# Loading bands earlier and reordering the blocks of V in a neighbourhood-attention kernel

## The chip, the cores and the metric

The kernel runs on one core of a Trainium2 chip. The metric is device time in microseconds of one execution, as the median of several runs. Five engines run their own instruction streams in program order: TensorE (PE, with its weight loads as PEld), VectorE (DVE), ScalarE (ACT), GpSimd (POOL) and SyncE (SP), which here does nothing but issue DMAs. ACT and POOL issue some DMAs as well.

## The reference

```python
H = W = 224; C = 192; ks, dil = 7, 2
qkv = x @ wqkv                       # x: 224 x 224 x 192, bf16
q, k, v = qkv[..., :C], qkv[..., C:2*C], qkv[..., 2*C:]
r0 = clip(i - 6, 0, H - 1 - 12); c0 = clip(j - 6, 0, W - 1 - 12)
rows, cols = r0 + 2 * arange(7), c0 + 2 * arange(7)
logits = einsum('bnc,bnkc->bnk', q, k[rows, cols]) * C ** -0.5
o = einsum('bnk,bnkc->bnc', softmax(logits), v[rows, cols]) @ wo
```

Each pixel attends to 7 x 7 neighbours at a distance of two rows and two columns. So pixels of one row parity and one column parity form an image of their own, 112 x 112.

## The kernel before

**Steps and pairs.** There are 14 steps `n`, numbered from 0: seven row tiles `ti` of 16 rows by two row classes `rc` (`rc = n % 2`). Each step has 7 pairs `m` of column slots `s = 2m, 2m + 1`, so 98 pairs `k` in all. A pair goes through stages: `stage1` (logits on TensorE, L500; the row maxima on VectorE, L502), `stage1b` (the exponentials on ScalarE, L510), `stage2` (transposes of the probabilities, L529, copied by L530), `stage3` (probabilities times V, L539) and `stage4` (reciprocal L545, scaling L562 into a tile `o_sb`, and the store, L568). In the loop body of pair `k`, `stage3` and `stage4` are those of pair `k - 2`. There are six `o_sb` tiles and each pair writes two.

**Preparation.** While step `n` runs, its pairs also prepare step `n + 1`: the folded queries `G` (`g_items`, L424, evacuated by L334 and on the GpSimd side by L459) and the 14 blocks of V, two a pair (`v_item`, L341 and L344, the cast by `evac`, L334 on ScalarE or L332 on VectorE). A block is 8 columns of a row class.

**VF and VD.** `VF[rc]` holds V of two bands of 8 rows on its lower and upper 64 partitions. `VD[rc]` holds the band before and the lower one. It is filled by DMAs from `VF`: `vd_low` (L355) copies the old upper half of VF to the lower half of VD, and must have read it before new blocks are cast over it; `vd_high` (L358) copies the new lower half of VF to the upper half of VD. `AT` says in which place of the tiles each block lies, so that one DMA can take neighbouring places. Before, blocks 0 to 6 lie at places 0 to 6, block 13 at 7 and blocks 7 to 12 at 8 to 13. In steps 1 to 12 `vd_low` of the other class goes out as seven blocks in pair 1, and `vd_low` of the own class as four and three blocks in pairs 4 and 5. `vd_high` goes out after the eighth block (pair 3) and after the last (pair 6).

**Loads.** `load_items(b)` brings band `b` of x (16 image rows) in three transposing DMAs (L155): two into the rings `XA`, one into `X1`, which has two buffers. Before, in pair 0 of step `n` band `n + 3` is put in `ld`, and each of the pairs 0, 1 and 2 issues one of its three. GpSimd then copies the band into `XB` (`xb_items`) and sorts it into strips `XS` (`sort_items`), from which the blocks of V are made.

**Order.** Everything is emitted by hand in program order and kept so on each engine (`in_order`). SP's queue takes, in a pair, the stores of `stage4`, then `vd_low`, then a load, then `vd_high`. SP issues one DMA after the other; one whose data are not ready holds up those behind it. The DMAs of SP and ACT use eight completion semaphores in turn, so each waits for the DMA eight before it. Step 0 follows a written `PLAN` (V: blocks of its own V, W: blocks of the next step, G and H: queries, R and T: `vd_high`, N: the second `stage4` of a pair, X: `xb_items`). In step 0 the `vd_high` marked `Ta` and the `vd_low` of pairs 4 and 6 are issued by ACT. Step 0 also has transfers of marks in pairs 3 to 6 (`marks_on`, L240).

Of the kernel before, what the change touches and what calls it, by code (L numbers as in the profile page):

```python
# [22 lines left out]
NSTEP = 14  # L23
NBAND = 14
# [3 lines left out]
BND = 16 * S  # L28
C = 192
VP = 2 * C + 2  # L30
AT = (0, 1, 2, 3, 4, 5, 6, 8, 9, 10, 11, 12, 13, 7)
NEG = -1.0e30


# [33 lines left out]
def _win(t, p0, pn, off, dims):  # L68
    a = t[:]
    ps = a.ap[0][0]  # L70
    return bass.AP(a.tensor, a.offset + p0 * ps + off, [[ps, pn]] + [list(d) for d in dims])
# [28 lines left out]
def kernel(  # L100
# [7 lines left out]
    nc = tc.nc  # L108
# [26 lines left out]
    VF = [pers.tile([128, NSLOT, VP], BF, name=f"vf{rc}") for rc in range(2)]  # L135
    VD = [pers.tile([128, NSLOT, VP], BF, name=f"vd{rc}") for rc in range(2)]
# [9 lines left out]
    def load_items(b):  # L146

        src = xp[16 * b:16 * b + 16].rearrange("r j c -> (r j) c")
        at = (16 * b) % (2 * RP) * S

        def one(k):
            if k == 1:
                X1[b] = x1_p.tile([128, BND], BF, name=f"x1_{b}", tag="x1")
            dst = X1[b][:] if k == 1 else XA[k // 2][:, at:at + BND]
            nc.sync.dma_start_transpose(out=dst.unsqueeze(1), in_=src[:, 128 * k:128 * k + 128])  # L155

        return [lambda k=k: one(k) for k in ((0, 2, 1) if b in (0, 2, 3) else (1, 0, 2))]

    def xb_items(b, eng):
        at = (16 * b) % (2 * RP) * S  # L160
# [46 lines left out]
    for cc in range(2):  # L207
        t = pers.tile([128, S], BF, name=f"ch{cc}")
# [121 lines left out]
    def evac(out_, in_, dve):  # L330
        if dve:
            nc.vector.tensor_copy(out=out_, in_=in_)  # L332
        else:
            nc.scalar.copy(out=out_, in_=in_)  # L334
# [11 lines left out]
    def v_item(rc, cb):  # L346
        def emit(dve):
            pv = ps_g.tile([128, 512], F32, name="pv", tag="pg")
            v_mms(pv, lambda k, h: XS[rc][:, k, cb, 64 * h:64 * h + 64])
            evac(_win(VF[rc], 0, 128, AT[cb] * VP, [[193, 2], [1, C]]), pv[:, 0:2 * C].rearrange("p (t c) -> p t c", c=C), dve)  # L350
        return emit

    def vd_low(rc, c0, c1, eng=nc.sync):

        eng.dma_start(out=VD[rc][0:64, c0:c1, 0:VP - 1], in_=VF[rc][64:128, c0:c1, 0:VP - 1])  # L355

    def vd_high(rc, c0, c1, eng=nc.sync):
        eng.dma_start(out=VD[rc][64:128, c0:c1, 0:VP - 1], in_=VF[rc][0:64, c0:c1, 0:VP - 1])  # L358


    def v_first(j):
        def emit(dve):
            pv = ps_g.tile([128, 512], F32, name="pv", tag="pg")
            v_mms(pv, lambda k, h: _win(XS[1], 0, 128, k * NSLOT * 128 + 64 * AT.index(2 * j + h), [[1, 64]]))
            evac(_win(VF[1], 0, 128, (7 + j) * VP, [[193, 2], [1, C]]), pv[:, 0:2 * C].rearrange("p (t c) -> p t c", c=C), dve)
        return emit

    def first_sort(eng):
# [1 line left out]

    def first_vd():
        for u in range(2):
            nc.sync.dma_start(out=_win(VD[1], 0, 64, u * VP, [[2 * VP, 7], [1, VP]]), in_=VF[1][64 * u:64 * u + 64, 7:14, :])


    def row_runs(rc, ti):
# [155 lines left out]
    def stage3(J, ab):  # L532
# [3 lines left out]
        for cc in range(2):  # L536
            for q in range(2):
                for h in range(2):
                    nc.tensor.matmul(o_ps[64 * h:64 * h + 64, cc * 193:cc * 193 + 193], lhsT=J.pt[:, 4 * ab + 2 * cc + q, 64 * h:64 * h + 64],  # L539
                                     rhs=V[h][:, AT[(s - 1 + q) % NSLOT], cc * C:cc * C + 193], start=(q == 0), stop=(q == 1))  # L540
        J.o_ps[ab] = o_ps
# [53 lines left out]
    for n, (ti, rc) in enumerate(steps):  # L595
        for m in range(7):
            J = Pair()
# [4 lines left out]
    def g_all(n):  # L602
# [3 lines left out]

    act, dve, pool = nc.scalar.copy, nc.vector.tensor_copy, nc.gpsimd.tensor_copy
    PLAN = (
        "Va:0 Vd:1 Va:2 Vd:3 Va:4 Vd:5 Va:6 Vd:7 R-:0:8 Va:8 Gd:2 Ga:3 X-",
        "Va:9 Vd:10 X- Va:11 Vd:12 Va:13 R-:8:14 Gd:4 Ga:5",  # L610
        "Gd:6 N- Ga:7 Wa:0 Wd:1 Wa:2",
        "Hd:0 N- Ha:1 Wa:3 Wa:4 Wd:5",
        "Hd:2 N- Ha:3 Wa:6 Wa:7 Ta:0:8 Wd:8",
        "Hd:4 N- Ha:5 Wa:9 Wa:10 Wd:11",
        "Hd:6 N- Ha:7 Wa:12 Wa:13 Ta:8:14",
    )
    pool_q = []
    end_q = []
# [11 lines left out]
    for it in load_items(2):  # L630
        it()
# [11 lines left out]
    t = ps_t.tile([128, 8, 128], BF, name="pt_ps", tag="pt")  # L643
# [13 lines left out]
    ld = []  # L657

    for k in range(NP + 2):
        J = pairs[k] if k < NP else None  # L660
        n = J.n if J else NSTEP
        w64, w128 = [], []
        if J:
            m = J.m
            if m == 0 and n + 1 < NSTEP:
                rc1 = steps[n + 1][1]
                gw, gh = g_all(n + 1)
                vs = [v_item(rc1, cb) for cb in (0, 1, 2, 3, 4, 5, 6, 13, 7, 8, 9, 10, 11, 12)]
            if n == 0:
                w64 = (gh0 + gh)[m + 1:m + 2]  # L670
            elif n + 1 < NSTEP:
                w128 = gw[m + (m > 1):m + 1 + (m > 0)] + vs[2 * m:2 * m + 2]
                w64 = gh[m // 2:m // 2 + 1] if m % 2 == 0 else []
            stage1(J, 0)
            stage1(J, 1)
            stage1b(J, 0)
            if m == 0 and n + 3 < NBAND:
                ld = load_items(n + 3)
        if k == NP:
            stage2(pairs[k - 1])  # L680
        if k >= 2:
            stage3(pairs[k - 2], 0)
            stage3(pairs[k - 2], 1)
            if k >= NP:
                stage4a(pairs[k - 2], 0)
                stage4a(pairs[k - 2], 1)
            stage4(pairs[k - 2], 0)
            if k == NP - 1:
                stage4a(pairs[k - 2], 1)
        for it in w64:  # L690
            it(False)
        if J:
            stage1b(J, 1)
        if 1 <= k < NP:
            stage2(pairs[k - 1])

        if k >= 2 and n > 0:
            stage4(pairs[k - 2], 1)
        if not J:
            continue  # L700

        if m == 1 and 0 < n and n + 1 < NSTEP:
            vd_low(rc1, 7, 14)
        if n == 0 and m in (4, 6):
            vd_low(0, *((0, 4) if m == 4 else (4, 7)), nc.scalar)
        if 0 < n and m in (4, 5) and n + 2 < NSTEP:
            vd_low(J.rc, *((0, 4) if m == 4 else (4, 7)))
        if ld:
            ld.pop(0)()
        for w in PLAN[m].split() if n == 0 else ():  # L710
            (kind, by), at = w.split(":")[0], [int(c) for c in w.split(":")[1:]]
            if kind in "VWGH":
                {"V": v0, "W": vs, "G": gw0, "H": gw}[kind][at[0]](by == "d")
            elif kind == "N" and k >= 2:
                stage4(pairs[k - 2], 1)
            elif kind == "X":
                xb2.pop(0)()
            elif kind == "R":
                vd_high(0, at[0], at[1], nc.scalar if by == "a" else nc.sync)
            elif kind == "T":  # L720
                vd_high(rc1, at[0], at[1], nc.scalar if by == "a" else nc.sync)
        for it in w128:
            it(False)
            if it is vs[7]:
                vd_high(rc1, 0, 8)
            if it is vs[13]:
                vd_high(rc1, 8, 14)
        if n == 0 and m == 0:
            for q in range(2):
                marks(q, 2 * MM, 2 * MM + 3, pool)  # L730
        if n == 0 and m == 1:
            first_vd()
            g_row_on(1, 2, 12)
            g_col_on()
        if n == 0 and m >= 3:
            marks_on(m % 2, 2 * MM + 3 + (m - 3) // 2)
        add = []
        if n == 0:
            add = {0: sort_items(1, 1, pool), 1: sort_items(2, 1, pool), 3: sort_items(2, 0, pool), 4: xb_items(3, pool) + sort_items(3, 0, pool)}.get(m, [])
        else:  # L740
            if m == 0 and n + 2 < NBAND:
                add = sort_items(n + 2, J.rc, pool)

            if m in ((2, 4) if n > 1 else (3,)) and n + 3 < NBAND:
                srt = sort_items(n + 3, J.rc, pool)
                one, two = xb_items(n + 3, pool) + srt[2:], srt[:2]
                add = (two if m == 4 else one) if n > 1 else one + two
        pool_q[:0] = add
        if n == 1 and m == 1:
            g_col(0, 1, 0, 1, pool)  # L750
            g_row(0, 1, 0, 1, pool, ((0, 16, MM - 6, 1),))
            g_row(0, 1, 1, 13, pool, ((0, 6, MM - 6, 1),))
        if n == 12 and m == 1:
            last = ((0, 9, 0, 1), (9, 7, 9, 0))
            g_col(1, 6, 0, 1, pool)
            g_row(1, 6, 0, 1, pool, last)
            g_row(1, 6, 1, 13, pool, last[1:])
        pool_do(5 if n == 1 and m == 3 else 4)
# [34 lines left out]
```

## Time and profile before

| | us |
|---|---|
| median of 3 runs | 360.83 |
| the runs | 360.83, 363.97, 360.31 |
| the profiled execution | 362.43 |
| its span | 360.7 |
| PE, PEld busy | 332.8, 302.4 |
| DVE, ACT, POOL busy | 314.0, 312.3, 281.0 |
| DMA moved | 60.05 MB, mean 167 GB/s |

The span runs from the first to the last instruction; the profiled execution's own time is 1.7 us more. Busy time is that of an engine's own work, and matmuls are pipelined, so that TensorE's busy time isn't TensorE at its peak. A group of instructions carries the line of kernel.py that issued it; `evac` and the stages are helpers, so one line stands for many places in the loop. SPq is SP's queue of DMA issues.

### The profile page before, as it was taken

The page shows a single profiled execution, that of the slowest core. Times are in us where ns is not written, and L with a number is a line of the kernel's source. Part 1 is how long each engine was busy: PE and PEld are TensorE (multiplying, and loading weights), DVE is VectorE, ACT ScalarE, POOL GpSimd, SP SyncE. Part 2 cuts the span into 40 slices and gives each one's busy share as a digit, 9 for nine tenths or more (in the row PEclk, how much of TensorE's full clock was granted, in tenths as well). Part 3 has the DMA queues.
Part 4 walks back from the last instruction along what each step waited for, and adds up shares of the span by engine and source line. Part 5 has one row for each costly group of instructions (what it writes and reads, how often), then busy time and mean ns, then how long its engine had stood idle before and what let it go on. Part 6 is the DMA issues. An engine that isn't in the chain of part 4 may idle for free.

```text
span 360.7 us, 18676 instructions
## 1 busy us (share of the span) xinstructions
PE 332.8 (92%) x7714; PEld 302.4 (84%) x7714; DVE 314.0 (87%) x743; ACT 312.3 (87%) x825; POOL 281.0 (78%) x446
## 2 busy tenths in 40 slices
PE   4686999989999998999999999999999999999872
PEld 2575878879998897899987999889999999999762
DVE  8977999878998888789987899898998989989893
ACT  7854779799999896999989999999999989999893
POOL 8595799999996977959959699696996878274182
PEclk9998999999999999999999999999999999999999
DMA  8997776899978969889699897998979955645423
GB/s 192 210 175 110 172 169 162 142 209 191 182 160 183 195 153 179 204 165 192 154 175 207 170 208 177 205 188 200 202 171 199 176 136 118 151 97 121 101 66 91
DMA packets 136768, 60.05 MB, mean 167 GB/s; under 512 B 88706, under 2 KB 136159, under 8 KB 136684
## 3 DMA queue, kind: packets, MB, share of 16 engines
q1 hardware_dynamic: 129412, 55.73, 76.1%
q0 software_dynamic: 5280, 1.71, 2.7%
q10 hardware_dynamic: 1992, 1.44, 2.0%
q8 instruction: 60, 0.98, 1.2%
q14 instruction: 24, 0.20, 0.1%
HBM read 0.29 MB, written 19.27 MB: 54 GB/s over the span
## 4 chain that ended last, share of the span: by engine, by line
PE 69%; DVE 11%; ACT 10%; DMA 4%; issue 4%; DVEq 0%; ACTq 0%
PE s L500 16%; PE o_ps L539 13%; PE pg L424 9%; PE pv L341 9%; PE pt_ps L529 8%; PE pv L344 7%; ACT p L510 7%; PE pgh L424 5%; DMA vd<-vf 4%; DVE nmx L502 3%; DVE o_sb L562 2%; ACT gx L334 1%; ACT g L334 1%; DVE g L332 1%; DVE pt_sb L530 1%
## 5 line engine op out<-in xcount | busy, mean ns | idle before, releaser
L510 ACT ACTIVATE p<-s,nmx 128x224 bf16<-128x224 f32 x392 | 150.9, 455 | 22.3 <-DVE nmx L502 20.3
L502 DVE TENSOR_REDUCE nmx<-s 128x2 f32<-128x392 f32 (+1 forms) x196 | 102.6, 565 | 21.0 <-PE s L500 19.5
L459 POOL COPY g<-gx 64x512 bf16<-64x512 bf16 (+1 forms) x110 | 62.3, 566 | 48.1 <-ACT gx L334 44.2
L334 ACT CAST vf<-pv 128x384 bf16<-128x384 f32 x193 | 88.6, 528 | 12.5 <-DMA vd<-vf 8.1
L562 DVE TENSOR_TENSOR o_sb<-o_ps,rs 128x384 bf16<-128x384 f32 x169 | 94.2, 558 | 5.9
L591 POOL DMA_DIRECT2D out_dram<-o_s x150 | 84.6, 571 | 9.4 <-DVE rs L545 7.8
L341 PE MATMUL pv<-wb,xs 128*64 128x384 bf16 x406 | 72.7, 333 | 14.0 <-ACT gx L334 5.5
L539 PE MATMUL o_ps<-vd,pt_sb 128*64 128x193 bf16 x784 | 81.6, 246 | 2.3 <-ACT pt_sb L530 2.1
L500 PE MATMUL s<-xa,g 128*64 128x196 bf16 (+7 forms) x990 | 82.6, 233 | 1.2 <-ACT p L510 0.7
L500 PE MATMUL s<-xb,g 128*64 128x196 bf16 (+7 forms) x990 | 82.3, 233 | 0.3 <-ACT g L334 0.3
L539 PE MATMUL o_ps<-vf,pt_sb 128*64 128x193 bf16 x784 | 81.7, 246 | 0.0
L500 PEld LDWEIGHTS <-g 128*64 128x64 bf16 x1980 | 78.1, 111 | 3.2 <-issue 1.6
L539 PEld LDWEIGHTS <-pt_sb 128*64 128x64 bf16 x1568 | 71.3, 109 | 3.8 <-ACT pt_sb L530 3.1
L344 PE MATMUL pv<-wp,xs 128*64 128x192 bf16 x812 | 73.0, 249 | 0.0
L530 DVE COPY pt_sb<-pt_ps 128x1024 bf16<-128x1024 bf16 x92 | 63.2, 687 | 5.7 <-PE pt_ps L529 0.6
L344 PEld LDWEIGHTS <-xs 128*64 128x64 bf16 x812 | 60.1, 111 | 8.2
L529 PE MATMUL pt_ps<-ident,p 128*64 128x128 bf16 x1552 | 63.8, 219 | 0.0
L529 PEld LDWEIGHTS <-p 128*64 128x64 bf16 x1552 | 57.1, 110 | 4.9
L334 ACT CAST g<-pg 128x512 bf16<-128x512 f32 (+4 forms) x136 | 58.0, 474 | 2.5 <-PE pg L424 2.3
L424 PEld LDWEIGHTS <-aw 128*64 128x64 bf16 x1320 | 55.2, 111 | 3.3
L424 PE MATMUL pg<-xb,aw 128*64 128x512 bf16 (+9 forms) x440 | 54.9, 271 | 0.0
L341 PEld LDWEIGHTS <-xs 128*64 128x64 bf16 x406 | 33.7, 111 | 23.3 <-issue 14.4
(77 smaller groups left out, 383.8 us busy)
## 6 DMA issues: line engine op xcount, KB each, us to landing
out_dram<-o_sb SPq DMA_DIRECT2D x156, 96.0 KB
vd<-vf SPq DMA_DIRECT2D x13, 385.0 KB
vd<-vf SPq DMA_DIRECT2D x12, 336.9 KB
vd<-vf SPq DMA_DIRECT2D x13, 288.8 KB
vd<-vf SPq DMA_DIRECT2D x11, 192.5 KB
vd<-vf SPq DMA_DIRECT2D x11, 144.4 KB
out_dram<-o_s POOLq DMA_DIRECT2D x78, 9.0 KB, 3.1
out_dram<-o_sb SPq DMA_DIRECT2D x13, 78.0 KB
```

Of the source, the lines that this page charges most:

```text
L334: nc.scalar.copy(out=out_, in_=in_)
L341: nc.tensor.matmul(pv[64 * h:64 * h + 64, 0:2 * C], lhsT=at(1, h), rhs=WB[:].rearrange("p t c -> p (t c)"), start=True, stop=False, skip_g ...
L344: nc.tensor.matmul(pv[64 * h:64 * h + 64, cc * C:(cc + 1) * C], lhsT=at(2 * cc, h), rhs=WP[(cc, 0)], start=False, stop=True, skip_group_ch ...
L424: nc.tensor.matmul(o, lhsT=l, rhs=r, start=(pas == 0), stop=(pas == 1))
L500: nc.tensor.matmul(o, lhsT=w, rhs=r, start=(pas == 0), stop=(pas == 1))
L502: nc.vector.tensor_reduce(out=nmx[:], in_=_win(s_ps, 0, 128, lo, [[256, 2], [16, 14], [1, 16 - lo]]), axis=AX.XY, op=ALU.max, negate=True)
L510: nc.scalar.activation(out=J.p[:, ab, cc, :, z:z + 112].rearrange("p q (r k) -> p q r k", k=8), in_=_win(s_ps, 0, 128, cc * 256, [[8, 2], ...
L529: nc.tensor.transpose(pt_ps[64 * h:64 * h + 64, 4 * ab + 2 * cc + q, :], J.p[:, ab, cc, q, 64 * h:64 * h + 64], ident[:])
L530: (nc.scalar.copy if J.n == NSTEP - 1 and J.m < 5 else nc.vector.tensor_copy)(out=J.pt[:], in_=pt_ps[:])
L539: nc.tensor.matmul(o_ps[64 * h:64 * h + 64, cc * 193:cc * 193 + 193], lhsT=J.pt[:, 4 * ab + 2 * cc + q, 64 * h:64 * h + 64], rhs=V[h][:, A ...
L562: nc.vector.tensor_tensor(out=o_sb[:], in0=_win(o_ps, 0, 128, 0, [[194, 2], [1, C]]), in1=rs[:].unsqueeze(2).to_broadcast([128, 2, C]), op ...
L591: pool_q.append(lambda dst=dst, p=p, m=n * nj, cc=cc: nc.gpsimd.dma_start(out=dst.rearrange("j i c -> i j c"), in_=o_sb[p:p + m, cc, :]))
```

## The change

The blocks of V are placed anew: 7 to 12 at places 0 to 5, block 13 at place 6, and 0 to 6 at places 7 to 13. Block 7 is made in pair 3 and block 13 in pair 4, where it was block 13 and then block 7. `vd_low` of the other class goes out in two parts, four blocks (7 to 10) in pair 0 and three (11 to 13) in pair 1. The first `vd_high` goes out after the ninth block, in pair 4.

Band `n + 4` is loaded in step `n`, in pairs 2, 3 and 6; pairs 4 and 5 issue no load. At the start, step 0 loads band 3 as before and puts band 4 in pairs 5 and 6 of step 0 and pair 0 of step 1. The transpose into `X1` comes last of the three for all bands but band 1.

```diff
-AT = (0, 1, 2, 3, 4, 5, 6, 8, 9, 10, 11, 12, 13, 7)
+AT = (7, 8, 9, 10, 11, 12, 13, 0, 1, 2, 3, 4, 5, 6)
...
-        return [lambda k=k: one(k) for k in ((0, 2, 1) if b in (0, 2, 3) else (1, 0, 2))]
+        return [lambda k=k: one(k) for k in ((1, 0, 2) if b == 1 else (0, 2, 1))]
...
-            evac(_win(VF[1], 0, 128, (7 + j) * VP, [[193, 2], [1, C]]), pv[:, 0:2 * C].rearrange("p (t c) -> p t c", c=C), dve)
+            evac(_win(VF[1], 0, 128, j * VP, [[193, 2], [1, C]]), pv[:, 0:2 * C].rearrange("p (t c) -> p t c", c=C), dve)
...
-        "Va:0 Vd:1 Va:2 Vd:3 Va:4 Vd:5 Va:6 Vd:7 R-:0:8 Va:8 Gd:2 Ga:3 X-",
-        "Va:9 Vd:10 X- Va:11 Vd:12 Va:13 R-:8:14 Gd:4 Ga:5",
+        "Va:0 Vd:1 Va:2 Vd:3 Va:4 Vd:5 Va:6 Vd:7 R-:6:14 Va:8 Gd:2 Ga:3 X-",
+        "Va:9 Vd:10 X- Va:11 Vd:12 Va:13 R-:0:6 Gd:4 Ga:5",
...
-        "Hd:2 N- Ha:3 Wa:6 Wa:7 Ta:0:8 Wd:8",
+        "Hd:2 N- Ha:3 Wa:6 Wa:7 Wd:8 Ta:6:14",
...
-        "Hd:6 N- Ha:7 Wa:12 Wa:13 Ta:8:14",
+        "Hd:6 N- Ha:7 Wa:12 Wa:13 Ta:0:6",
...
-                vs = [v_item(rc1, cb) for cb in (0, 1, 2, 3, 4, 5, 6, 13, 7, 8, 9, 10, 11, 12)]
+                vs = [v_item(rc1, cb) for cb in (0, 1, 2, 3, 4, 5, 6, 7, 13, 8, 9, 10, 11, 12)]
...
-            if m == 0 and n + 3 < NBAND:
-                ld = load_items(n + 3)
+            if n == 0 and m == 0:
+                ld = load_items(3)
+            if n == 0 and m == 5 or n > 0 and m == 2 and n + 4 < NBAND:
+                ld = load_items(n + 4)
...
-        if m == 1 and 0 < n and n + 1 < NSTEP:
-            vd_low(rc1, 7, 14)
+        if m in (0, 1) and 0 < n and n + 1 < NSTEP:
+            vd_low(rc1, *((4, 7) if m else (0, 4)))
         if n == 0 and m in (4, 6):
-            vd_low(0, *((0, 4) if m == 4 else (4, 7)), nc.scalar)
+            vd_low(0, *((7, 11) if m == 4 else (11, 14)), nc.scalar)
         if 0 < n and m in (4, 5) and n + 2 < NSTEP:
-            vd_low(J.rc, *((0, 4) if m == 4 else (4, 7)))
-        if ld:
+            vd_low(J.rc, *((7, 11) if m == 4 else (11, 14)))
+        if ld and not (n > 0 and m in (4, 5)):
             ld.pop(0)()
...
-            if it is vs[7]:
-                vd_high(rc1, 0, 8)
+            if it is vs[8]:
+                vd_high(rc1, 6, 14)
             if it is vs[13]:
-                vd_high(rc1, 8, 14)
+                vd_high(rc1, 0, 6)
```

`first_vd` reads places 0 to 6 of `VF[1]` in place of 7 to 13 in the same way.

More of the change, by code (lines that the diff above doesn't have):

```diff
@@ L372, in first_vd @@
         for u in range(2):
-            nc.sync.dma_start(out=_win(VD[1], 0, 64, u * VP, [[2 * VP, 7], [1, VP]]), in_=VF[1][64 * u:64 * u + 64, 7:14, :])
+            nc.sync.dma_start(out=_win(VD[1], 0, 64, u * VP, [[2 * VP, 7], [1, VP]]), in_=VF[1][64 * u:64 * u + 64, 0:7, :])
     def row_runs(rc, ti):
```

## Prediction

> **What bounds the kernel now.** I read the page first: busy times and the chain that ended last.
>
> ```profile
> PE 332.8 (92%) x7714; PEld 302.4 (84%) x7714; DVE 314.0 (87%) x743; ACT 312.3 (87%) x825; POOL 281.0 (78%) x446
> PE 69%; DVE 11%; ACT 10%; DMA 4%; issue 4%; DVEq 0%; ACTq 0%
> ACT vf L334 <- DMA vd<-vf: 8.1, 4, 3.0
> ```
>
> The third line is from the list of waits: microseconds, times, longest. TensorE sets the pace. The 4% of DMA in the chain can't be taken as the gain, since a transfer's whole flight is counted there; so I cut the trace at the first row maximum (L502) of each step and read the windows.
>
> ```profile
> 57.11:81.66 24.55, 22.77 (x500) 20.41 (x497) 20.59 (x49) 20.52 (x57) 23.86 (x42) 1.00 0.86 174
> 81.66:104.08 22.42, 22.37 (x500) 20.42 (x497) 20.56 (x50) 21.17 (x58) 21.74 (x32) 1.00 0.99 187
> 104.08:127.22 23.14, 22.58 (x500) 20.50 (x497) 20.58 (x50) 21.05 (x58) 19.80 (x28) 1.00 0.88 178
> 127.22:152.38 25.16, 23.21 (x577) 21.83 (x574) 20.66 (x49) 21.26 (x59) 20.28 (x30) 1.00 0.91 178
> ...
> 175.24:198.97 23.73, 22.81 (x551) 19.78 (x547) 20.55 (x50) 21.02 (x58) 18.93 (x27) 1.00 0.91 178
> 198.97:221.37 22.40, 22.35 (x500) 20.31 (x496) 20.55 (x49) 21.24 (x58) 18.49 (x26) 1.00 0.96 187
> ...
> 266.19:288.99 22.80, 22.80 (x577) 21.73 (x574) 20.63 (x49) 21.46 (x59) 17.40 (x25) 1.00 0.87 182
> ```
>
> Columns: stretch, length, then busy PE, PEld, DVE, ACT, POOL. Seven steps show, 1 to 4, 6, 7 and 10. Steps 2, 7 and 10 have PE busy all but 0.05 us: that is the floor, 22.41 us, or 22.80 for a step with the matmul count of step 10. Four steps are longer: step 1 by 24.55 - 22.41 = 2.14, step 3 by 0.73, step 4 by 25.16 - 22.80 = 2.36, step 6 by 1.32; together 6.55 us. ScalarE's timeline shows what happens in step 1, and SP's why:
>
> ```profile
> 69.36 0.52 ACT L334 CAST vf<-pv 128x384 bf16<-128x384 f32 x1
> 72.66 0.48 ACT L334 CAST vf<-pv 128x384 bf16<-128x384 f32 x1 [2.79 <-DMA vd<-vf]
> ```
> ```profile
> 52.99 2.54 SPq L568 DMA_DIRECT2D out_dram<-o_sb  x3
> 55.58 0.64 SPq L240 DMA_DIRECT2D xb<-xb  x1
> 56.33 2.85 SPq L568 DMA_DIRECT2D out_dram<-o_sb  x3
> 59.24 0.79 SPq L240 DMA_DIRECT2D xb<-xb  x1
> 60.13 2.53 SPq L568 DMA_DIRECT2D out_dram<-o_sb  x3
> 62.76 1.92 SPq L155 DMA_TRANSPOSE x<-in_x_dram  x1
> 64.78 2.54 SPq L568 DMA_DIRECT2D out_dram<-o_sb  x3
> 67.41 0.67 SPq L355 DMA_DIRECT2D vd<-vf  x1
> ```
>
> The cast that waits is block 13 of V, second in pair 3. It overwrites what the seven-block shift of L355, of pair 1, still reads. That shift goes out at 67.41 and takes 5.17 us to land (its row in the chain; 5.45 and 4.92 in steps 4 and 6). It goes out late because SP issues back to back: every row above starts as the one before ends. About 0.65 us of a wait is absorbed: 2.79 cost 2.14, and the 3.02 of step 4 cost 2.36.
>
> **The change, part by part.** Only SP's sequence of operations changes, and gains one shift a step; PE, DVE, ACT and POOL do the same operations in the same order on other blocks. The blocks' new places move the same bytes in rows of the same length: 0.
>
> *Steps 3, 4 and 6.* Block 13 is cast one pair later but first of its two: 2.93 - 0.48 = 2.45 us of margin. The load that stood ahead of the shift in pair 0 (1.88, median of the X1 transposes) is gone, and a four-block shift (0.62 + 0.08) stands there: +1.2. Three blocks land sooner than seven: 4 blocks are 192.5 KB, at some 175 GB/s in these windows 1.1 us. Together 4.7 us against a longest wait of 3.0, so these three lose 0.73 + 2.36 + 1.32 = 4.41 us. Bounds: 0 (SP late by 4.7 us more) and 4.41. I take 4.41.
>
> *Step 1.* Here the queue gets worse. Two transposes of band 4 now go out in pairs 5 and 6 of step 0, into the stretch shown above, which has no gap. One costs SP 1.33 to 3.65 us (L155), near here 1.65 (at 41.96) and 1.92; I take 1.75 + 0.1 each, 3.7 together. With the four-block shift ahead (0.7), the three-block shift leaves at 67.41 + 3.7 + 0.7 = 71.8 and lands 5.2 - 1.1 = 4.1 later, at 75.9 (73.9 if as fast as POOL's smallest stores, 2.1; 77.0 at the full 5.2). Block 13 would be cast at 69.36 + 2.93 = 72.3. Wait 3.6, cost 3.6 - 0.65 = 2.95 (1.0 to 4.0), in place of 2.14. Block 7, second of pair 3, needs the four-block shift by 69.88; that leaves at 66.5 and lands near 70.9: 1.0 of wait, 0.35 of cost, which the later wait contains.
>
> *The transfers ScalarE issues in step 0.* In the built program the three-block shift of pair 6 (L355) waits, on a DMA semaphore used in turn by eight, for another store than before: the one inside SP's run of 48.29, whose last count the trace has at 55.00. ScalarE reached this issue at 54.45. Behind it stand the exponentials of L510 at 54.84, and behind them TensorE: 0.55 us (0 if TensorE has slack, 1.0 at most with the issue's own 0.60 in line). The upper shift of pair 4 (L358) now waits for VectorE's cast, which ends at 48.60 instead of going at 48.22; ScalarE is idle until 49.10 anyway: 0, and 0.4 without that cover.
>
> *Store buffers.* Six o_sb tiles are written two a pair, so one is reused after three pairs, 3.43 + 3.36 + 2.90 = 9.7 us. A store lands 3.8 us after issue (median of L568's answer), so SP may issue it 5.3 us after the write's end. In step 1 the write of 68.10 to 68.66 is stored at 74.36, 5.7 later, without a wait. With 4.4 us more in the queue and 2.95 given back by the wait above, up to 1.5 us of a new wait can arise on VectorE at the turn to step 2, or none, as SP runs empty there. Nearest is the row without a wait; I take 0.5.
>
> *The loads themselves.* POOL's waits for loads (4.2 and 4.2 us) go, but POOL isn't in the chain: 0; without that cover 1 us. XA's places are free: nothing reads the band that is overwritten after the step before.
>
> SP's share is what the sum hangs on. The Trainium skill, "DMA: Bandwidth & Descriptors", section "Issuing engines are not separate DMA queues", says that the time to start a DMA is usually small against the DMA itself. Here the trace disagrees for transposes: 2.57 us of issue (median, XA) against flights of about 5. By the Trainium skill's rule the queue of step 1 would hold nothing up and the time would be that of the first rival below.
>
> **Sum**, against the profiled execution's 362.43 us (span 360.7 and 1.7 around it): 362.43 - 4.41 - 2.14 + 2.95 + 0.55 + 0.5 = 359.9. Its floor without any of the waits is 362.43 - 6.55 = 355.9. The runs' median is 360.83, 1.6 below the profiled one, which I read as other runs having shorter waits, not a lower floor. So the forecast is 0.3% under the median.
>
> **Rivals.** (a) *All four waits go and none comes*: 355.9. For it: from step 10 on SP issues stores right behind their writes, so it has time to spare, and a 1.65 us transpose in step 0 may partly use time in which SP waits for o_sb. Against it: the gapless rows above. (b) *The stores become the wait*, slower. SP issues one more transfer a step (six shifts, not five), transposes in pairs 2 and 3 stand directly ahead of three shifts in pairs 4 and 5, and the transpose of pair 6 stands ahead of the last upper shift. In step 4 the write that starts at 138.46 is stored at 144.43, 5.4 us after its end, which is already at the 5.3 allowed. With 0.7 more a step VectorE waits 5.4 + 0.7 - 5.3 = 0.8 us in each of the eight steps 2 to 9: 355.9 + 2.95 + 0.55 + 6.4 = 365.8. It decides from the point where the store is issued more than 5.3 us behind its write in every step that loads. Against it: in steps 7 to 9 that lag stays under 4 us, and no o_sb wait shows anywhere. (c) *It does not do what it says*: the short shift of pair 1 is still late in steps 3, 4 and 6, because SP's lag from step 1 carries on: about 362.
>
> **Chances.** Forecast 0.42, (a) 0.36, (b) 0.18, (c) 0.04. Over 1% is about what a measurement of this kernel can tell from no change: faster is (a), 0.36; same is the forecast and (c), 0.46; slower is (b), 0.18. The forecast's own range is 357.5 to 362.0 (step 1 at 1.0 or 4.0, stores 0 to 1.5). To hold 8 in 10 it goes down past (a) to 355.0 and up to 365.0, leaving out the upper part of (b).
>
> **What would show it.** Right: steps 3, 4 and 6 at 22.4, 22.8 and 22.4 us with no wait of L334 for vd; step 1 still over 24, with the first cast of pair 4 waiting for the second lower shift, and SP's issue of it near 72; 0.5 us more in the last pair of step 0. Wrong towards (a): step 1 at 22.4. Wrong towards (b): VectorE's L562 waiting for out_dram stores in most steps up to 9.

## The result and the profile after

The changed kernel takes 365.94 us (median of 6 runs, 364.64 to 367.64) against 362.16 for the kernel before in the same session: ratio 1.0111, 95% interval 1.0067 to 1.0155. It is slower by about 4 us, where 0.9 us faster had been forecast. Executions over 1.5% slower than the fastest of the same kernel and session are left out of all ratios.

The page of the changed kernel, its busy times and its chain; the profiled execution took 366.2 us, its span is 364.4:

```profile
PE 334.8 (92%) x7714; PEld 301.6 (83%) x7714; DVE 311.4 (85%) x743; ACT 312.0 (86%) x825; POOL 280.7 (77%) x446
PE 68%; DVE 11%; ACT 8%; DMA 7%; issue 4%; DVEq 0%; SPq 0%; ACTq 0%
```

Its list of waits (total us, times, longest):

```profile
DVE o_sb L562 <- DMA out_dram<-o_sb: 13.9, 13, 2.7
ACT vf L334 <- DMA vd<-vf: 5.6, 3, 2.5
```

The engines do the same work as before. The first line is new: in the profile before, no store was waited for. The second was 8.1 us in 4 waits. DMA's share of the chain went from 4% to 7%. The windows by step, columns as in the prediction (steps 1 to 6 and 10):

```profile
55.56:83.86 28.30, 24.52 (x508) 20.80 (x504) 20.06 (x49) 20.82 (x58) 27.55 (x48) 1.00 0.96 169
83.86:107.38 23.52, 22.36 (x486) 20.02 (x487) 20.23 (x50) 20.53 (x56) 19.70 (x28) 1.00 0.94 192
107.38:129.79 22.41, 22.36 (x500) 20.43 (x497) 20.55 (x50) 21.23 (x58) 18.85 (x27) 1.00 0.91 182
129.79:152.59 22.80, 22.80 (x577) 21.75 (x574) 20.61 (x49) 21.45 (x59) 18.34 (x27) 1.00 0.92 182
152.59:177.38 24.79, 23.49 (x628) 21.92 (x624) 20.75 (x50) 21.49 (x59) 20.08 (x29) 1.00 0.95 178
177.38:199.84 22.46, 22.41 (x552) 20.22 (x546) 20.54 (x49) 21.20 (x58) 18.01 (x26) 1.00 0.93 182
...
267.18:292.14 24.96, 23.79 (x577) 21.68 (x574) 20.19 (x49) 21.19 (x59) 18.38 (x26) 1.00 0.84 170
```

Against before: step 1 +3.75, step 2 +1.10, step 5 +1.93, step 10 +2.16; steps 3, 4 and 6 -0.73, -2.36 and -1.27. Step 0 ended 1.55 us sooner, and the tail after step 12 took 0.56 longer; with 0.13 in step 7 the sum is 3.7, the difference of the spans. Step 0 isn't the change's doing. In all profiled executions but one it takes 37.7 to 38.1 us where its granted clock is 0.95 or 0.96, as in the profile before, and 35.0 to 36.1 where it is 1.00, as in this one; a kernel below with the same step 0 as the changed one (the one with a single shift) has 37.77 at 0.95. A step 1 that starts at 57.1 has left SP some 1.5 us more to catch up than one that starts at 55.6, so a window of step 1 is to be read with its start.

SP's timeline shows step 1 being made late:

```profile
52.51 1.64 SPq L568 DMA_DIRECT2D out_dram<-o_sb  x2
54.20 1.96 SPq L155 DMA_TRANSPOSE xa<-in_x_dram  x1
...
60.70 1.69 SPq L155 DMA_TRANSPOSE xa<-in_x_dram  x1
62.50 0.83 SPq L568 DMA_DIRECT2D out_dram<-o_sb  x1
63.38 1.06 SPq L240 DMA_DIRECT2D xb<-xb  x1
64.55 2.68 SPq L568 DMA_DIRECT2D out_dram<-o_sb  x3
67.32 0.65 SPq L355 DMA_DIRECT2D vd<-vf  x1
68.06 2.28 SPq L155 DMA_TRANSPOSE x<-in_x_dram  x1
70.44 2.56 SPq L568 DMA_DIRECT2D out_dram<-o_sb  x3
73.09 0.66 SPq L355 DMA_DIRECT2D vd<-vf  x1
```

Who pays for it stands in the timelines of VectorE and ScalarE (in brackets the idle time before, and what ended it):

```profile
73.99 0.56 DVE L562 TENSOR_TENSOR o_sb<-o_ps,rs 128x384 bf16<-128x384 f32 x1 [2.48 <-DMA out_dram<-o_sb]
82.12 0.56 DVE L562 TENSOR_TENSOR o_sb<-o_ps,rs 128x384 bf16<-128x384 f32 x1 [2.67 <-DMA out_dram<-o_sb]
89.94 0.56 DVE L562 TENSOR_TENSOR o_sb<-o_ps,rs 128x384 bf16<-128x384 f32 x1 [2.04 <-DMA out_dram<-o_sb]
```
```profile
70.54 0.48 ACT L334 CAST vf<-pv 128x384 bf16<-128x384 f32 x1 [1.64 <-DMA vd<-vf]
75.89 0.86 ACT L334 CAST vf<-pv 128x384 bf16<-128x384 f32 x2 [2.54 <-DMA vd<-vf]
```

Step 5 is a case of its own: only 0.2 us of store wait is listed there, and TensorE's longest idle time, 1.10 us, is one that the profile gives to nothing that it shows:

```profile
158.25 0.30 PE L529 MATMUL pt_ps<-ident,p 128*64 128x128 bf16 x4 [1.10 <-issue]
```

Elsewhere the shifts wait as forecast; the stores wait too, most of them in other pairs. The waits add, but not in full: the 11.3 us of them in step 1 (7.1 for stores, 4.2 for shifts) put it 5.9 us over its floor. A number that will be used below is SP's *lag*: the start of a store on SP less the end of the write on VectorE that it stores, worked out from the trace for each tile (of a tile stored in two parts, for the first). In step 1 its median is 2.9 us before (longest 5.7) and 7.8 us after (longest 10.1); over steps 1 to 9 it is 2.4 before and 4.0 after.

### The profile page after: what moved, and what is told of

It reads as the page before. It is cut to its first block, busy times and chain, and to the rows that moved or that the text cites. A ratio compares the mean times of both kernels' runs of the same rounds, so it can differ in the third digit from the quotient of the medians.

```text
span 364.4 us, 18700 instructions
## 1 busy us (share of the span) xinstructions
PE 334.8 (92%) x7714; PEld 301.6 (83%) x7714; DVE 311.4 (85%) x743; ACT 312.0 (86%) x825; POOL 280.7 (77%) x446
## 4 chain that ended last, share of the span: by engine, by line
PE 68%; DVE 11%; ACT 8%; DMA 7%; issue 4%; DVEq 0%; SPq 0%; ACTq 0%
PE s L500 15%; PE o_ps L539 14%; PE pg L424 9%; PE pt_ps L529 9%; PE pv L341 9%; PE pv L344 7%; DMA out_dram<-o_sb 7%; PE pgh L424 5%; ACT p L510 5%; DVE nmx L502 3%; DVE o_sb L562 2%; DVE pt_sb L530 2%; DVE g L332 1%; ACT g L334 1%; ACT pt_sb L530 1%
## 5 line engine op out<-in xcount | busy, mean ns | idle before, releaser
L562 DVE TENSOR_TENSOR o_sb<-o_ps,rs 128x384 bf16<-128x384 f32 x169 | 94.2, 557 | 19.4 <-DMA out_dram<-o_sb 13.9
L539 PE MATMUL o_ps<-vd,pt_sb 128*64 128x193 bf16 x784 | 82.8, 246 | 6.9 <-DVE pt_sb L530 2.9
L539 PE MATMUL o_ps<-vf,pt_sb 128*64 128x193 bf16 x784 | 82.9, 247 | 0.0
L539 PEld LDWEIGHTS <-pt_sb 128*64 128x64 bf16 x1568 | 71.3, 109 | 10.1 <-DVE pt_sb L530 3.7
L344 PEld LDWEIGHTS <-xs 128*64 128x64 bf16 x812 | 59.9, 111 | 8.9 <-issue 0.5
L529 PEld LDWEIGHTS <-p 128*64 128x64 bf16 x1552 | 57.1, 110 | 6.5 <-issue 1.6
L424 PE MATMUL pg<-xa,aw 128*64 128x512 bf16 (+9 forms) x440 | 52.3, 270 | 0.0
```

The lines of the kernel that those rows point to most:

```text
L344: nc.tensor.matmul(pv[64 * h:64 * h + 64, cc * C:(cc + 1) * C], lhsT=at(2 * cc, h), rhs=WP[(cc, 0)], start=False, stop=True, skip_group_ch ...
L424: nc.tensor.matmul(o, lhsT=l, rhs=r, start=(pas == 0), stop=(pas == 1))
L529: nc.tensor.transpose(pt_ps[64 * h:64 * h + 64, 4 * ab + 2 * cc + q, :], J.p[:, ab, cc, q, 64 * h:64 * h + 64], ident[:])
L562: nc.vector.tensor_tensor(out=o_sb[:], in0=_win(o_ps, 0, 128, 0, [[194, 2], [1, C]]), in1=rs[:].unsqueeze(2).to_broadcast([128, 2, C]), op ...
```

## The experiments

Two theories were set up first: S, that six store tiles are too few, and Q, that SP's queue is late and whichever buffer is shortest waits. Later a third came in: D, that the DMA engines behind the queue are full. Each expectation speaks of the theories as they stood when its kernel ran.

**The change taken apart.** First the placing and order of V's blocks with the split shifts, and the loads as before:

```diff
-AT = (0, 1, 2, 3, 4, 5, 6, 8, 9, 10, 11, 12, 13, 7)
+AT = (7, 8, 9, 10, 11, 12, 13, 0, 1, 2, 3, 4, 5, 6)
 ... all else of the change but load_items, ld and its pop
```

> The new places of the blocks, the new order (block 7, then 13) and the lower shift in two parts, with the loads left as they were before. Theory S (the loss of the changed kernel is VectorE's wait for a free store tile, because SP's queue, with loads put earlier, issues the stores late): the casts' wait for the shift (8.1 us before) falls below 1 us, no wait for stores over 1 us comes, and the time is 356 to 358 us, 1 to 1.8% under the kernel before. Rival R (the sixth shift a step, or the new order of blocks, is what costs): 364 us or more, with waits for stores spread over the steps.

359.83 us, ratio 0.9976 (0.9943 to 1.0009): no difference shown. Its waits say why:

```profile
DVE o_sb L562 <- DMA out_dram<-o_sb: 8.0, 10, 2.1
ACT vf L334 <- DMA vd<-vf: 0.3, 1, 0.3
```

The shift's 8.1 us of waits are gone as planned, and 8.0 us of store waits stand in their place. The lag over steps 1 to 9 is 3.6 in place of 2.4.

Then the loads alone, V as before:

```diff
-            if m == 0 and n + 3 < NBAND:
-                ld = load_items(n + 3)
+            if n == 0 and m == 0:
+                ld = load_items(3)
+            if n == 0 and m == 5 or n > 0 and m == 2 and n + 4 < NBAND:
+                ld = load_items(n + 4)
 ... and the change's order in load_items and its pop
```

> The new loads alone, on the old places, the old order and one lower shift of seven blocks in pair 1. Theory S: two transposes in step 0 put SP behind by 4 us, so step 1 waits both for the shift (block 13 is now cast a pair sooner than in the changed kernel) and for store tiles: step 1 is 28 us or longer, and the time 365 to 369 us. Rival R: about the time of the kernel before, 361 to 363 us, since the loads are only moved.

369.66 us, ratio 1.0213 (1.0121 to 1.0305), with 13.7 us of shift waits and 4.9 of store waits; step 1 took 32.11 us. So the loads are what costs, some 7.7 us alone. With the V part as well it is 4.0, but the two intervals overlap (1.0067 to 1.0155 and 1.0121 to 1.0305), so that the V part takes some of it back isn't shown.

**More store tiles.** Eight `o_sb` tiles in place of six: first in the changed kernel, with one `o_s0` fewer, then with both `o_s0` kept and room made elsewhere (one constant tile for two, one `gx` fewer), then that same edit in the kernel before and in the V part alone.

```diff
-            o_sb = work.tile([128, 2, C], BF, name="o_sb", tag="o_sb", bufs=6)
+            o_sb = work.tile([128, 2, C], BF, name="o_sb", tag="o_sb", bufs=8)
```

> The changed kernel with eight store tiles o_sb in place of six (paid for with two gx tiles in place of three and one o_s0 in place of two). Theory S: VectorE's wait for stores falls from 13.9 us to under 3, the wait of the casts for the shift in step 1 stays at 3 to 6, and the time is 357 to 360 us. Rival R, or a limit in the DMA engines themselves: the wait moves but the time stays at 364 to 366.

> The changed kernel with eight store tiles o_sb in place of six and two gx tiles in place of three; both o_s0 tiles are kept (the earlier run with one o_s0 met a wait of 10 us for it in step 1, which hid what was asked). Theory S: no wait of VectorE for stores over 1 us in all, in place of 13.9; the casts still wait 2 to 5 us for the shift in step 1; time 357 to 360 us. Rival B (the transfers are late because the DMA engines are full, and the wait turns up at another place): 363 to 366.

> The kernel before with the same eight o_sb and two gx tiles: the control. It has no wait for store tiles, only the casts' wait for the shift, so theory S expects no gain: within 1% of the kernel before, 359 to 363 us. If two gx tiles cost anything it shows here.

> The part of the change that concerns V alone (places, order, lower shift in two parts; loads as before) with eight o_sb and two gx tiles. Theory S: both waits are gone, the 8.1 us of the casts and the 8.0 us for stores that the V part alone showed, so every step from 1 on runs at 22.4 or 22.9 us and the time is 353 to 356 us, under both kernels. Rival B: 358 to 361, as the V part alone.

Measured 1.0154 (1.0073 to 1.0236), 1.0197 (1.0136 to 1.0258), 1.0030 (0.9996 to 1.0065) and 0.9999 (0.9956 to 1.0042). Theory S falls: nothing comes back. In the profiled execution of the first (371.63 us, the longest of its four), the single `o_s0` became a wait of its own, 10.0 us at one place in step 1. What waits in the second isn't known, as its profile is the one left out above. In the last no `o_sb` waits, but the shift does:

```profile
ACT vf L334 <- DMA vd<-vf: 4.2, 5, 1.1
```

Its lag grows to medians of 6.4 and 6.6 us in steps 6 and 7, where the V part with six tiles has 3.0. More tiles let SP fall further behind, until the shifts in the same queue are what is late.

**Other places for the transposes, one shift in place of two.** The changed kernel without transposes in pairs 5 and 6 of step 0 (band 4 in pairs 0 to 2 of step 1, band 5 in pairs 3 and 6 and pair 0 of step 2):

```diff
-            if n == 0 and m == 0:
-                ld = load_items(3)
-            if n == 0 and m == 5 or n > 0 and m == 2 and n + 4 < NBAND:
+            if m == 0 and n < 2:
+                ld = load_items(n + 3)
+            if n == 1 and m == 3 or n > 1 and m == 2 and n + 4 < NBAND:
```

> The changed kernel without loads in pairs 5 and 6 of step 0: band 4 is loaded in pairs 0, 1 and 2 of step 1 as before the change, band 5 in pairs 3 and 6 of step 1 and pair 0 of step 2, and the rest as changed. Theory S with the start as its cause: steps 1 and 2, 28.30 and 23.52 us in the changed kernel, come down to 24 and 23 at most, and the time is 360 to 362. Rival: if the loads ahead in every step are what makes the stores late, waits for stores show in most steps and the time stays over 364.

Then the changed kernel with the lower shift of pairs 0 and 1 as one of seven blocks, and both edits together:

```diff
-        if m in (0, 1) and 0 < n and n + 1 < NSTEP:
-            vd_low(rc1, *((4, 7) if m else (0, 4)))
+        if m == 1 and 0 < n and n + 1 < NSTEP:
+            vd_low(rc1, 0, 7)
```

> The changed kernel with the lower shift of the other class as one transfer of seven blocks in pair 1 again, five shifts a step in place of six. Theory S with SP's issues as its cause: 0.7 us less a step in SP's queue, the waits for stores fall from 13.9 to some 8 us, but block 7, cast in pair 3, waits for the shift as block 13 did before, above all in step 1: 363 to 367 us, about the changed kernel. Rival R (it is the sixth transfer that costs): the time of the kernel before or less, 358 to 362.

> The changed kernel with both suspected costs taken away at once: no transposes in pairs 5 and 6 of step 0 (the fourth band is loaded in pairs 0 to 2 of step 1, the fifth in pairs 3 and 6 of step 1 and pair 0 of step 2), and the lower shift again as one seven-block transfer in pair 1. Theory Q (SP's issue queue is late for two separate reasons: the early loads spoil step 1, and the sixth shift of each step spoils the steps that load): step 1 near 22.6 us as without the early loads, and steps 2 to 10 near 22.4 and 22.8 as with one shift, so 355.5 to 358.5 us, ratio to the kernel before 0.985 to 0.994. Rival (the two costs are one: a queue that is late by a given amount, which one of the two edits merely moves from step 1 to the later steps): the loads that went to step 1 take the place of the shift saved, store waits of 5 us or more remain in steps 2 to 6, time 361 to 364.

Measured 1.0111 (1.0073 to 1.0148), 1.0190 (1.0162 to 1.0218) and 1.0125 (1.0064 to 1.0186). The loss moves and stays. Without the transposes in step 0, steps 1 and 2 are

```profile
57.12:79.69 22.57, 22.53 (x504) 20.58 (x501) 20.39 (x49) 20.88 (x58) 21.68 (x39) 1.00 0.86 173
79.69:104.09 24.40, 22.78 (x496) 20.12 (x493) 20.20 (x50) 20.89 (x58) 20.00 (x29) 1.00 0.98 195
```

so step 1, which starts at 57.12 here, is nearly clean, but each of the steps 2 to 9 is 0.3 to 2.0 us over its floor. With one shift, the debt is paid at once, in step 1, and step 2 and nearly all behind it are clean (step 7 is 1.3 us over its floor):

```profile
57.06:88.42 31.36, 25.27 (x500) 22.56 (x497) 20.92 (x50) 20.68 (x57) 30.25 (x52) 0.89 0.99 183
88.42:110.82 22.40, 22.36 (x500) 20.43 (x497) 20.55 (x50) 21.20 (x58) 16.98 (x24) 1.00 0.85 176
```

With both edits the wait moves to step 2 (28.22 us, a cast waiting 5.6 us for the shift). I had expected these two causes to be separate and to vanish together, 355.5 to 358.5; that was wrong.

**One more shift alone.** The kernel before, its shift of pair 1 in two parts, one behind the other:

```diff
-            vd_low(rc1, 7, 14)
+            vd_low(rc1, 7, 11)
+            vd_low(rc1, 11, 14)
```

> The kernel before with one edit: the seven-block lower shift of pair 1 goes as two transfers (four and three blocks), one right behind the other, so SP issues one transfer more in each step and nothing else moves. Theory Q: the sixth transfer costs SP some 0.7 us a step; it shows as store waits (of L562) or longer shift waits in the steps that load, 1 to 4 us over the kernel. Rival (the sixth transfer by itself is free; what costs is that shifts now stand in pairs 0 and 1 ahead of the stores): no store wait, the short second shift lands sooner than seven blocks, time equal to the kernel before or up to 1.5 us under it.

359.41 us, 0.9988 (0.9953 to 1.0023), shift waits 3.2 and store waits 2.2. So no cost of the sixth transfer by itself is shown.

**Other queues.** The upper shifts of steps 1 to 11 issued by ScalarE, in the changed kernel and in the V part alone:

```diff
-                vd_high(rc1, 6, 14)
+                vd_high(rc1, 6, 14, nc.scalar)
...
-                vd_high(rc1, 0, 6)
+                vd_high(rc1, 0, 6, nc.scalar)
```

> The changed kernel, with the two upper shifts (L358) of steps 1 to 11 issued by ScalarE, so SP has two transfers fewer in each of these steps while the DMA engines move the same bytes. Theory Q (it is SP's issue queue that is late): store waits of 13.9 us fall under 5, the part of them in steps 2 to 10 all but gone; step 1 gets shorter by 1 to 3 us; against that stands about 0.6 us of ScalarE's time for each issue, 22 of them, of which some reaches the path; 359 to 364 us. Rival (the DMA engines are what is late, not the issue): store waits stay at 10 us or more and the time is 366 or longer.

> The kernel before with the V part alone (blocks in the new places, shifts split), loads as before, and the upper shifts of steps 1 to 11 issued by ScalarE. With SP issuing these it had 8.0 us of store waits and 359.8 us. Theory Q: SP then has four shifts a step, one fewer than before the change; store waits under 2 us, steps 1, 4, 9 and 11 back near 22.4 and 22.8 us, 355.5 to 358.5 us. Rival (the DMA engines, or the loads that POOL waits for): time stays at 359 to 361, as ScalarE's issues cost what the stores give.

1.0283 (1.0204 to 1.0363) and 1.0123 (1.0070 to 1.0176), both slower. In the first, 7.7 us of store waits remain. In the second, they fell from 8.0 to 4.9 us, all in step 1, but steps 3, 7, 8 and 9 are 22.96 to 22.98 us where the floor is 22.41, and steps 4, 5, 6 and 10 are 0.2 to 0.5 us over theirs: two issues on ScalarE cost up to 0.57 us a step, more than SP's relief returns.

Three stores a step issued by POOL, in the changed kernel and in the kernel before:

```diff
-                    put(nc.gpsimd if nj < 8 and s % 2 == 1 else nc.sync)
+                    put(nc.gpsimd if nj < 8 and s % 2 == 1 or 0 < J.n < 11 and s % 4 == 3 else nc.sync)
```

> The changed kernel, in which three stores of each of the steps 1 to 10 (those of slots 3, 7 and 11) are issued by POOL instead of SP. The bytes are the same. Theory Q (SP's issue queue is late): at the 0.46 us an issue that the tiny copies cost, three a step are 1.4 us of relief a step, 13.7 in all, against 13.9 us of store waits: these fall under 4, steps 2 to 10 are at 22.4 and 22.8, step 1 still at 23 to 26 as its debt is 5 us; 356.5 to 360 us. Theory D (the DMA engines are late whoever issues): store waits stay at 10 us or more, 364 to 367. A third way (POOL is late with these stores, behind its copies, and the tiles come free late): store waits in the pairs of slots 3, 7 and 11, 364 or more.

> The kernel before with the same three stores of each of the steps 1 to 10 issued by POOL. Theory Q: SP runs ahead of its 0.65 us of margin, the waits of steps 1, 3, 4 and 6 for the shift (8.1 us) fall under 3, and the time is 355.5 to 358.5 us. Theory D: no change, 359 to 362. Where POOL is late with these stores, store waits appear that the kernel before does not have, and the time is 361 or more.

1.0133 (1.0096 to 1.0170) and 1.0045 (1.0012 to 1.0079). In the first, steps 3 to 8 are at 0 to 0.3 us over their floors (step 5 is 22.92, where the changed kernel has 24.79), step 9 at 1.0, and step 10 at 22.79 (24.96), so the later part of the loss does hang on SP's share. But steps 1 and 2 are 27.73 and 26.08 us, and 11.8 us of store waits remain: the longest, 2.98 us at 90.26, is for a tile whose store SP issued at 83.14, 6.8 us after its write, and which landed at 90.17, a flight of 7 us where the median is 4.0. There it was the transfer as well as the issue. In the second the shift's waits fell from 8.1 to 2.9 us, as theory Q said, but 3.9 us of store waits came in their place, and both are for tiles whose store POOL issued, 6.2 and 7.9 us after the write. So the way that the expectation names last came true, and this kernel doesn't say what a relieved queue is worth.

**The price by itself.** The kernel before with two transposes more, in pairs 5 and 6 of step 0 (the first two of band 4, which is loaded again at its old place):

```diff
                 ld = load_items(n + 3)
+            if n == 0 and m == 5:
+                ld = load_items(4)[:2]
```

> The kernel before with two transposes added and nothing else: the first two of band 4 are issued in pairs 5 and 6 of step 0, as in the changed kernel, and all of band 4 is loaded again at its old place. It measures the disputed cost by itself. Theory D (two transposes in the full stretch cost their DMA time, 2.5 to 3.3 us each, once): 4 to 7 us over the kernel before, 365 to 368, nearly all of it in steps 1 and 2. Rival (the prediction's step 1: 3.7 us more in the queue make a wait of 3.6 in place of 2.8): 0.8 us over, 361 to 362. A third reading (the early loads cost only in company with the split shifts and the new order of blocks): equal to the kernel before.

364.93 us, ratio 1.0128 (1.0069 to 1.0188): two transposes cost 4.6 us (2.5 to 6.8), about as much as the whole change. Steps 1 and 2:

```profile
55.56:87.26 31.70, 24.98 (x500) 22.16 (x497) 20.75 (x50) 20.55 (x57) 29.77 (x51) 0.89 0.98 175
87.26:109.66 22.40, 22.36 (x500) 20.41 (x497) 20.56 (x49) 21.23 (x58) 17.63 (x25) 1.00 0.90 191
```

Of the 4.6 us, some 2.2 are TensorE's slower clock in step 1 (0.89, with 24.98 us of matmul time for 22.77 before), which the changed kernel doesn't have; so 4.6 and 4.0 aren't one price measured twice. Its lag in step 1 is 8.1 us (longest 9.7), about that of the changed kernel, and 0.5 to 1.1 in steps 2 to 4. It also has steps 3 and 4 at 22.41 and 22.80, with no edit of V: the stall of step 1 let SP catch up.

Next, one more issue in every pair of steps 1 to 10, with next to no bytes:

```diff
+    ticks = [pers.tile([16, 32], BF, name=f"tick{q}") for q in range(4)]
...
+        if 0 < n < 11:
+            nc.sync.dma_start(out=ticks[J.k % 4][:], in_=ident[0:16, 0:32])
```

> The kernel before with one more issue on SP in every pair of steps 1 to 10: a copy of 16 rows of 64 bytes, 70 issues in all, seven a step, which by the nearest row (0.6 us an issue) are 4.3 us of SP's time a step, with a thousandth of the bytes. Theory Q (the number of issues on SP is the bound): each of the steps 1 to 10 gets 2 to 4 us longer, 385 us or more. Theory D (the DMA engines are the bound, and SP's issues stretch or shrink with them): at most a few us more, 361 to 366, most of it where shifts stand behind one more issue.

391.86 us, ratio 1.0893 (1.0830 to 1.0956): some 32 us for 70 issues, 0.46 each. In the profiled execution some 13 of the 33 us by which steps 1 to 10 grew are TensorE's: it was busy for 239.6 us in them, where it was 226.5 before, as the clock fell to 0.94 in seven of them. The shift is what waits, with every one of the steps 1 to 10 longer; the list of waits and step 2 (the lines of kernel.py are one further here):

```profile
ACT vf L335 <- DMA vd<-vf: 36.5, 11, 5.2
```
```profile
84.83:111.29 26.46, 24.40 (x500) 21.83 (x497) 20.92 (x49) 21.13 (x58) 21.24 (x31) 0.94 0.77 164
```

The DMA engines are less busy than before (0.77 where step 2 had 0.99), a store of SP lands 3.4 us after its issue, as before, and SP still has no gap. Theory D, which said 361 to 366, falls in this form: once SP is full, issues cost by their number too, 0.68 us of SP's time for each copy.

Then the reverse, the changed kernel with the same issues and fewer bytes (the SP stores of steps 0 to 9 write the first half of their rows, the other half is left out of the output):

```diff
-                def put(eng, j0=j0, nj=nj, r0=r0, rstep=rstep):
+                def put(eng, j0=j0, nj=(nj + 1) // 2 if J.n < 10 else nj, r0=r0, rstep=rstep):
```

> The changed kernel, in which the stores of L568 up to step 9 write only the first half of their rows (half of that part of the output is left out): the same number of issues on SP, some 0.5 MB less a step to move. Theory D: store waits all but gone, step 1 near 22.6 to 24, steps 2 to 10 at 22.4 and 22.8; 355 to 358 us. Theory Q: SP issues as many transfers as before, so waits of 8 us or more remain and the time stays at 362 to 366.

359.29 us, ratio 0.9982 (0.9950 to 1.0013): the whole loss is gone, so Q in its plain form (362 to 366) falls too. Its store waits and step 1:

```profile
DVE o_sb L562 <- DMA out_dram<-o_sb: 1.4, 2, 1.1
```
```profile
57.13:79.54 22.41, 22.36 (x500) 20.41 (x497) 20.57 (x50) 20.71 (x57) 21.78 (x39) 1.00 0.84 168
```

The lag in step 1 is 5.3 us and about 1 from step 5 on, over steps 1 to 9 1.5 in place of 4.0; a store's flight is 3.4 us at the median in place of 4.0 (3.4 in the kernel before). This step 1 starts at 57.13, so its window alone would show less than the 12 times do.

Last the opposite direction, the V part alone with the loads one pair later from step 2 on:

```diff
-            if m == 0 and n + 3 < NBAND:
+            if m == (n > 1) and n + 3 < NBAND:
...
-            if m in ((2, 4) if n > 1 else (3,)) and n + 3 < NBAND:
+            if m in ((3, 4) if n > 1 else (3,)) and n + 3 < NBAND:
```

> The kernel before with the V part alone (places, order, split shifts), and from step 2 on the loads one pair later (pairs 1, 2 and 3 rather than 0, 1 and 2; POOL's copies of the band in pair 3 rather than 2). Theory D (what is brought forward costs, so what is put off gives back): the 8.0 us of store waits of the V part alone fall to 4 or less and the time is 356 to 359 us, under both kernels. Rival (POOL's copies come late and hold up TensorE, or the order of SP's queue matters and not the demand): 360 us or more.

360.55 us, 1.0016 (0.9978 to 1.0054). Store waits fell to 4.2 us in the profile, but the time didn't follow; its profiled execution, 357.4, was the fastest of twelve. No version tried is shown to beat the kernel before.

**What the runs settle.** SP's queue is full, and how much fits into it hangs on the number of transfers and on their bytes. By the trace of before, SP's issues with the 0.09 us between them fill 97 to 100% of each of the steps 1 to 9, 93% of step 10 and 63% of step 11. Added issues cost (the small copies), fewer bytes give back (the half stores), and fewer issues on SP clear the later steps (three stores to POOL in the changed kernel). A store's issue is 0.54 us at best and 2.14 at worst, and with half stores SP's issues of steps 1 to 10 took 195 us in place of 212. That issues stretch when the engines are behind fits this, but isn't shown by itself. The eight completion semaphores aren't the cause: in steps 1 to 9 the earlier transfer on the same semaphore had landed at least 1.4 us before each issue of SP before the change, and at least 1.0 after it, but for one issue (0.15).

In the versions tried, work put in front of this stretch came back as a stall; tiles, shifts and other places only chose which consumer stalled. The change's loss is 4.0 us (2.4 to 5.6). What the early loads save comes in step 10, with one transpose in place of three; that step was at its floor before. Not settled are the 1.93 us of step 5 in the changed kernel, which no wait in its list accounts for, how the 4.6 us of two transposes divide between issue, engines and clock, as fewer bytes made the issues shorter too, and what a queue with room would gain, as ScalarE and POOL paid for SP's relief.

## Why the prediction was wrong, by its steps

- **Steps 3, 4 and 6, -4.41.** They came to 22.41, 22.80 and 22.46 with no wait for vd, as said. But the credit didn't stay: steps 2, 5 and 10, which the sum left untouched, took back 1.10 + 1.93 + 2.16 = 5.2 us, in step 2 as store waits (2.0 us) and in step 10 as waits for stores (3.4) and for a shift (1.4). The V part alone shows it in one kernel, 8.1 us of shift waits for 8.0 of store waits. Nor does the credit belong to the new order alone, as two added transposes without it cleared steps 3 and 4 too.
- **Step 1, the shifts.** The issues were put at 66.5 and near 72 and came at 67.32 and 73.09; the waits of 1.0 and 3.6 were 1.64 and 2.54, and the cast of block 13 came at 75.89, where 75.9 was the landing forecast. This mechanism was right. That the two times agree to 0.01 us is luck: the shift went out over 1 us later than forecast and landed in 2.8 us, not 4.1.
- **Store buffers, +0.5: the step that failed.** The terms were there: 5.7 us of lag before and 4.4 us more in the queue, 10.1 us against the 5.3 allowed. But the prediction set the shift's 2.95 against the 4.4, as if that stall covered the stores, put the 1.5 left at the turn to step 2, and chose 0.5 because the nearest row had no wait. The stores came late in pairs 1 to 4 and 6 of step 1 as well, three of them before the shift's stall, and the stalls added in part: the store waits are 13.9 us in all, 7.1 of them in step 1 and 2.0 in step 2, and step 1 came out 5.9 us over its floor, where 2.95 was forecast. With 10.1 - 5.3 = 4.8 in place of 0.5 the sum would have been 364.2. That 10.1 is also the longest lag measured is luck: it is another tile's, and the store that had 5.7 before has 8.8.
- **The 3.8 us of flight behind the 5.3 allowed** were misread. L568's answer times only POOL's seven stores of 18 KB. Worked out from the semaphores in the traces, SP's stores land 3.4 us after issue at the median before and 4.0 after, and those behind the waits of 2.67 and 2.04 us took 5.3 and 6.5; so a longer flight is part of these waits.
- **"SP runs empty there."** The excess was taken to end at step 2. It lasts to step 10: the lag is 2.8 to 4.8 us in steps 2 to 9 and 1.0 in step 10, the first in which SP issues one transpose and not three.
- **ScalarE's transfers in step 0, +0.55.** The semaphore came 0.02 us before the issue, and the exponentials behind it start 0.48 us after the cast ahead of it in both traces, so this was 0.
- **The loads themselves, 0.** POOL wasn't in the chain, right, but the price of loads was looked for there and in one queue position, not as time that SP and the DMA engines must find.
- **The rival of the stores** (365.8) named the sign and the wait. That its size is near is luck: its even 0.8 us in each of the steps 2 to 9 is not what happened, as the long waits came in steps 1, 2 and 10. Its mechanism, one more transfer a step, isn't shown to cost anything alone (0.9988).
- **The Trainium skill's rule**, "DMA: Bandwidth & Descriptors", section "Issuing engines are not separate DMA queues", has two halves. That an issue is usually small beside its DMA doesn't hold for the transposes here, with 2.57 us of issue (median) against flights of about 5. That all engines' DMAs run on the same 16 DMA engines is tested by no run here alone: moved to ScalarE or POOL, issues brought no gain (1.0283, 1.0123, 1.0133, 1.0045), but ScalarE's time and POOL's lateness had their part in it.

## What to carry to other kernels

Before a transfer is moved forward, sum the issue times on its queue over the stretch it moves into; where they fill it, price the transfer at its full issue time as lost time, wherever the list of waits shows slack, and a stall that becomes long at more (below). A wait that goes from one buffer to another with its length kept is a sign that the queue is the bound and not the buffer. Follow every user of a late queue with its own margin and don't let the stall of one stand for the others'.

## What the runs showed of the hardware that was not expected

A long stall costs more than its length. With the two transposes added, a cast waited 6.5 us in step 1 and TensorE was idle for 4.8 us on end: the granted clock of that step was 0.89, and the 500 matmuls took 24.98 us of TensorE's time in place of 22.36. The shift as one transfer (wait of 7.5 us, TensorE idle for 5.7) shows 25.27 at 0.89. In the changed kernel, with waits up to 2.7 and TensorE idle for 1.2 at most, the clock of step 1 stayed at 1.00. The Trainium skill, "TensorE: Matmul & The Clock Gate", section "HAM oscillation — how this bites in real kernels", says that a gap of more than about 3.4 us without matmuls throttles the array. These three steps agree. The small copies don't: there idle times of TensorE of 1.3 and 1.4 us at most (steps 9 and 2) came with 0.94, and 1.6 us (step 10) with 1.00, so the length of the gap alone doesn't decide. In the trace of the small copies the clock is 0.50 from 75.83 to 79.24 us, behind the stall of step 1. So several short stalls can be cheaper than one long one, but no run here compares the two with all else equal.
